# Taking the attention output and its query gradient out of one PSUM bank with one multiply

## The chip, the core and the metric

The kernel runs on one core of a Trainium2 chip. Its engines work side by side, each through its own queue in order: TensorE (PE, with its weight loads PEld), VectorE (DVE), ScalarE (ACT), GpSimd (POOL), and SyncE (SP), which here only issues transfers. SBUF is the working memory and PSUM takes what TensorE writes; GpSimd works on SBUF. The metric is the time of one execution in microseconds, the median of the runs.

## The reference

Two attention blocks work on a sequence of 2048 tokens of width 448 with 16 heads of 28, and the program returns their joined output and the gradients of all eight inputs for a given gradient of the output. Block A is linear attention. Block B, with which the change deals, has one key head and one value head for all 16 query heads:

```python
q = (x @ wq).reshape(B, S, H, Dh).transpose(0, 2, 1, 3)
k, v = x @ wk, x @ wv
scores = einsum("bhqd,bkd->bhqk", q, k) * (Dh ** -0.5)
p = softmax(scores, axis=-1)
o = einsum("bhqk,bkd->bhqd", p, v)
out_B = o.transpose(0, 2, 1, 3).reshape(B, S, H * Dh) @ wo
```

Backward, with dO the gradient of o and D the sum of dO times o over a head's width: dP = dO v^T, dS = p (dP - D), dQ = scale dS k, dK = scale dS^T q, dV = p^T dO. The inputs are bfloat16.

## The kernel before, in words

After block A and the projections of block B, a core loop does the attention of block B forward and backward. Its work is cut into 64 blocks (`NB`), each of 256 queries (`qc`) and one pair of heads. A block has eight units of 256 keys; so there are 512 units (`NU`), and the loop at line 905 runs over `u` in 540 steps, 28 more than there are units because the backward stages trail. The heads are padded to 32 rows. The order of every engine's queue is the order in which the loop writes the instructions down (`tc.manual_schedule()`): it is set by hand, with `due(u, lag)`, which returns block b when u is 8 b + lag, and None otherwise.

In step `u`, in the order of the code:

- `rows_SD` (line 663): TensorE computes the scores S of unit u for both heads into two of three score banks (`SB`), and dP minus D for unit `w = u - 16` into the two banks `DB`. The third score bank is `spare`; which it is goes in a period of four steps (line 909). D comes in through an extra row: row 0 of a padded head of dO holds minus D over the softmax's sum, and v has minus ones there.
- For even u, `o_dq` advances two accumulations in one PSUM bank, `oq`: o of unit u-2 (`o_mm`, rows 0 to 63, with a row of ones in v that gives the softmax's sum) and dQ of unit u-20 (`dq_mm`, rows 64 to 127). A second call at the end of the step does units u-1 and u-19.
- The spare bank takes, by step, the transposes of o (`onat_T`, line 788), those of dO (`don_T`), or a part of the output projection (`out_proj`).
- ScalarE computes the first head's exponential (L927), copies the second head's dP to SBUF as `cp` (L941), and computes the second exponential (L973). VectorE multiplies the first head's dP by the exponential into `dsT` (L939), GpSimd does the same with `cp` for the second head (L942).
- VectorE's small work follows, and then, last in the step, a 32x32-block transpose of the `dsT` of two steps before (L1006), which the dK products read.
- SyncE transposes four units of exponentials at a time by a transfer, `eN<-eT` (L975), for the dV products (`dv_mm`); in the units 30 to 55 of every 64, GpSimd copies queries into `qst` (L833), and SyncE transposes those (L837). In odd steps TensorE runs the dK products (`dk_m`), in some even steps four dV products of `dv_mm`.

The chain of o through a block b, with the steps at which it is written down: VectorE copies rows 0 to 63 of `oq` to `oTs` at lag 9 (L955). TensorE transposes them through the spare bank at lag 10 (L791). `o_norm` at lag 10 takes the reciprocal of the softmax's sum (L800) and multiplies by it (L801), into the first 128 columns of `oTs`; GpSimd then multiplies by dO into `prod` (L805), scales dO into `don` (L808), and writes o as bfloat16 over dO in `do_nat` (L809). `row_D` at lag 12 sums `prod` on VectorE (L813), and GpSimd puts the result into `don` (L814). At lag 14 TensorE transposes `don` (L822), VectorE copies it to `doT` (L829), and at lag 16 the products of `rows_SD` begin to read it. dQ of a block is complete two blocks later; VectorE multiplies rows 64 to 127 of `oq` by the scale and writes them over the queries at lag 27 (L958). In units of a block (u modulo 8) the copy of o is thus in unit 1, the normalising in 2, the taking out of dQ in 3, the sum in 4, and the copy of `doT` in 6. The copy of a piece of the output projection (L728) is in unit 0.

Of the kernel before, what the change touches and what calls it, by code (L numbers as in the profile page):

```python
# [25 lines left out]
def kernel(  # L26
# [604 lines left out]
    with ExitStack() as cs_:  # L631
# [59 lines left out]
        identF = pp_.tile([P, P], F32, name="identF", bufs=1)  # L691
        make_identity(nc, identF[:])
        oTs = pp_.tile([P, 256], F32, name="oTs", bufs=1)
        wo = pc_.tile([P, 4, D], BF16, name="wo", bufs=1)
# [10 lines left out]
        outs.update({456 + 8 * n: (10 + n // 2, n % 2 * (D // 2), (n % 2 + 1) * (D // 2)) for n in range(8)})  # L705
# [76 lines left out]
        onps, tps2 = {}, {}  # L782
# [5 lines left out]
        def onat_T(b, bank):  # L788
            onp = bank[:, 0:P].rearrange("p (q h c) -> p q h c", q=2, h=2)
            for qb in range(2):  # L790
                nc.tensor.transpose(onp[:, qb, :, :].rearrange("p h c -> p (h c)"), oTs[0:64, qb * P:(qb + 1) * P],  # L791
                                    identF[0:64, 0:64], tile_position=(0, 0))
            onps[b] = onp

        def o_norm(b):
            onp = onps.pop(b)
            qc, pair, g, hp = blk(b)
            r_ = pw_.tile([P, 2, 2, 1], F32, name="rl")
            os_ = oTs[:, 0:P].rearrange("p (q h c) -> p q h c", q=2, h=2)
            nc.vector.reciprocal(out=r_[:], in_=onp[:, :, :, 0:1])  # L800
            nc.vector.tensor_tensor(out=os_, in0=onp[:, :, :, :], in1=r_[:].to_broadcast([P, 2, 2, 32]), op=ALU.mult)  # L801
# [3 lines left out]
            nc.gpsimd.tensor_tensor(out=prod[b][:], in0=dnv, in1=os_, op=ALU.mult)  # L805
            dn = pw_.tile([P, 2, 2, 32], BF16, name="don", bufs=3)
            don[b] = dn
            nc.gpsimd.tensor_tensor(out=dn[:], in0=dnv, in1=r_[:].to_broadcast([P, 2, 2, 32]), op=ALU.mult)  # L808
            nc.gpsimd.tensor_copy(out=dnv, in_=os_)  # L809
# [40 lines left out]
        def o_mm(v):  # L850
            b, tp = divmod(v, 8)
            for t2 in range(2):
                t = 2 * tp + t2
                for h in range(2):
                    mmt(oq[32 * h:32 * h + 32, 0:256], vaug[:, t, :],
                        eT(v)[:, h, t2 * 256:(t2 + 1) * 256], (0, 32 * h), t == 0, t == 15)
                yield

        def dq_mm(y):
            b, tp = divmod(y, 8)  # L860
            for t2 in range(2):
# [34 lines left out]
        with tc.manual_schedule():  # L896
# [8 lines left out]
            for u in range(NU + 28):  # L905
# [29 lines left out]
                if hasD:  # L935
# [5 lines left out]
                    nc.scalar.activation(out=cp[:, :], in_=dp[1][:, :], func=ACT.Copy)  # L941
                    nc.gpsimd.tensor_tensor(out=dst[:, 1, :], in0=cp[:, :], in1=ew[:, 1, :], op=ALU.mult)  # L942
                gq, iq = divmod(u % 64 - 30, 8)
                qq = u // 64 + 1
                if 0 <= gq < 4 and u < 448:
                    if gq == 0 and iq == 0:
                        qX[qq] = (pqb_ if qq % 2 else pqa_).tile([P, 4, 2, 512], BF16, name="qX")
                    if iq < 2:
                        qc_copy(nc.gpsimd, qst, qq, gq, iq)
                if (b := due(u, 12)) is not None:  # L950
                    row_D(b)
                if u == 7:
                    nc.vector.memset(oTs[64:128, :], 0.0)
                if (b := due(u, 9)) is not None:
                    nc.vector.tensor_copy(out=oTs[0:64, :], in_=oq[0:64, 0:256])  # L955
                if (b := due(u, 27)) is not None:
                    qc, pair, g, hp = blk(b)
                    nc.vector.tensor_scalar(out=qT_B[g][64 * hp:64 * hp + 64, qc * 256:(qc + 1) * 256],  # L958
                                            in0=oq[64:128, 0:256], scalar1=scale, scalar2=None, op0=ALU.mult)
# [162 lines left out]
```

## Time and profile before

| what | us |
|---|---|
| median of 3 runs | 1068.79 |
| lowest and highest run | 1068.59, 1069.49 |
| the profiled execution | 1067.99 |
| its span | 1066.3 |
| granted clock of TensorE in it | 0.998 |
| L939, first and last start | 240.2, 1016.8 |

The views are: the page, with the busy time of each engine and the chain of work that ended last; busy time by stretch; the waits, "who <- whom: us in total, times, longest"; and the timelines of single engines, with the start and duration of every instruction in us and in brackets the idle time before it and what ended it. On VectorE, ScalarE and GpSimd an instruction can start before the one in front has ended, since its first part overlaps the other's last; so the distance from start to start is what an instruction takes from its engine, and the durations are somewhat longer. TensorE's durations overlap far more, and its 98% say little.

### The profile page before, as it was taken

The page shows a single profiled execution, that of the slowest core. Times are in us where ns is not written, and L with a number is a line of the kernel's source. Part 1 is how long each engine was busy: PE and PEld are TensorE (multiplying, and loading weights), DVE is VectorE, ACT ScalarE, POOL GpSimd, SP SyncE. Part 2 cuts the span into 40 slices and gives each one's busy share as a digit, 9 for nine tenths or more (in the row PEclk, how much of TensorE's full clock was granted, in tenths as well). Part 3 has the DMA queues.
Part 4 walks back from the last instruction along what each step waited for, and adds up shares of the span by engine and source line. Part 5 has one row for each costly group of instructions (what it writes and reads, how often), then busy time and mean ns, then how long its engine had stood idle before and what let it go on. Part 6 is the DMA issues. An engine that isn't in the chain of part 4 may idle for free.

```text
span 1066.3 us, 39861 instructions
## 1 busy us (share of the span) xinstructions
PE 1042.2 (98%) x16241; PEld 476.1 (45%) x16241; DVE 896.1 (84%) x1797; ACT 873.7 (82%) x1741; POOL 781.3 (73%) x1033
## 2 busy tenths in 40 slices
PE   9999999999999999999999999999999999999998
PEld 5555555433444444444444444444444444444434
DVE  7888400459999999999999999999999999999943
ACT  6454122479999999999999999999999999999622
POOL 6001242227988898899889989988998999888881
PEclk9999999999999999999999999999999999999999
DMA  9749899079999999999999999999999999999963
GB/s 267 163 95 200 161 214 250 21 138 168 192 202 198 170 203 187 195 191 193 196 186 189 197 192 198 185 191 194 195 195 195 195 191 186 206 191 179 218 141 92
DMA packets 689936, 195.14 MB, mean 183 GB/s; under 512 B 670616, under 2 KB 687792, under 8 KB 689752
## 3 DMA queue, kind: packets, MB, share of 16 engines
q1 hardware_dynamic: 680152, 179.92, 99.2%
q0 software_dynamic: 4640, 8.71, 2.8%
q10 hardware_dynamic: 4960, 3.96, 1.3%
q8 instruction: 127, 2.08, 0.7%
q14 instruction: 57, 0.47, 0.1%
HBM read 12.60 MB, written 10.84 MB: 22 GB/s over the span
## 4 chain that ended last, share of the span: by engine, by line
PE 52%; DVE 35%; POOL 4%; issue 4%; ACT 3%; DMA 1%; DVEq 0%; POOLq 0%; ACTq 0%
PE agen L656 20%; PE agen L81 15%; DVE dsT L939 14%; DVE dsx L1006 12%; PE aacc L656 9%; PE aacc L81 7%; POOL dsT L942 4%; DVE R L958 2%; DVE oTs L801 2%; DVE oTs L955 2%; ACT cp L941 1%; DVE rl L800 1%; ACT eT L973 1%; DMA dsx<-R 1%; ACT eT L927 0%
## 5 line engine op out<-in xcount | busy, mean ns | idle before, releaser
L942 POOL TENSOR_TENSOR dsT<-cp,eT 128x512 bf16<-128x512 bf16 x512 | 588.1, 1157 | 77.3 <-ACT cp L941 68.9
L1006 DVE STREAM_TRANSPOSE dsx<-dsT 128x512 f32<-128x512 f32 x512 | 356.4, 696 | 2.4 <-POOL dsT L942 0.2
L656 PEld LDWEIGHTS <-R 32*128 32x128 bf16 (+1 forms) x9104 | 215.5, 93 | 318.3 <-issue 293.0
L939 DVE TENSOR_TENSOR dsT<-agen,eT 128x512 bf16<-128x512 f32 x512 | 338.5, 661 | 11.7 <-PE agen L656 8.4
L941 ACT ACTIVATE cp<-agen 128x512 bf16<-128x512 f32 x512 | 324.7, 634 | 12.5 <-PE agen L656 12.5
L927 ACT ACTIVATE eT<-aacc 128x512 bf16<-128x512 f32 x512 | 324.0, 633 | 11.6 <-PE aacc L656 4.7
L973 ACT ACTIVATE eT<-aacc 128x512 bf16<-128x512 f32 x512 | 330.6, 646 | 0.0
L656 PE MATMUL agen<-doT,R 32*128 32x256 bf16 x2048 | 270.9, 269 | 10.9 <-DVE dsT L939 8.2
L656 PE MATMUL aacc<-R,R 32*128 32x256 bf16 (+1 forms) x2240 | 269.7, 268 | 2.7 <-ACT eT L927 0.8
L656 PE MATMUL agen<-dsx,qX 32*32 32x512 bf16 x4096 | 267.7, 375 | 0.0
L656 PE MATMUL agen<-eT,R 128*32 128x256 bf16 x2048 | 182.0, 276 | 0.1
L656 PE MATMUL agen<-dsT,R 128*32 128x256 bf16 x2048 | 181.4, 276 | 0.1
L656 PEld LDWEIGHTS <-qX 32*32 32x32 bf16 x4096 | 79.7, 89 | 114.9 <-issue 54.3
L656 PE MATMUL aacc<-eN,don 128*32 128x512 bf16 x1024 | 97.6, 379 | 0.0
L81 PEld LDWEIGHTS <-R 128*128 128x128 bf16 (+1 forms) x517 | 41.0, 99 | 42.9 <-issue 11.1
L406 POOL COPY pk<-R 128x256 bf16<-128x256 bf16 x4 | 1.6, 397 | 75.3 <-DVE R L366 75.3
L81 PE MATMUL agen<-R,R 128*128 128x448 bf16 (+1 forms) x180 | 42.4, 363 | 0.3 <-ACT R L225 0.3
L833 POOL COPY qst<-R 128x512 bf16<-128x512 bf16 x56 | 34.2, 611 | 4.8 <-DMA qX<-qst 4.6
L805 POOL TENSOR_TENSOR prod<-R,oTs 128x128 f32<-128x128 bf16 x64 | 27.5, 430 | 9.8 <-DVE oTs L801 9.8
L656 PEld LDWEIGHTS <-don 128*32 128x32 bf16 x1024 | 34.2, 97 | 0.8
L422 DVE TENSOR_TENSOR osb<-aacc,pr 64x448 bf16<-64x448 f32 x2 | 1.2, 617 | 37.9 <-DMA out_dram<-osb 24.0
L958 DVE TENSOR_SCALAR R<-agen 64x256 bf16<-64x256 f32 x64 | 27.3, 426 | 3.6 <-PE agen L656 1.6
(231 smaller groups left out, 971.1 us busy)
## 6 DMA issues: line engine op xcount, KB each, us to landing
out_dram<-osb ACTq DMA_DIRECT2D x22, 112.0 KB
eN<-eT SPq DMA_TRANSPOSE x128
xa<-in_A_x_dram SPq DMA_DIRECT2D x8, 224.0 KB
ga<-in_grad_out_dram SPq DMA_DIRECT2D x4, 448.0 KB
xa<-in_grad_out_dram POOLq DMA_DIRECT2D x4, 448.0 KB, 5.7
out_dram<-wdq POOLq DMA_DIRECT2D x8, 224.0 KB, 3.8
eT<-in_grad_out_dram SPq DMA_DIRECT2D x4, 448.0 KB
eT<-in_B_x_dram SPq DMA_DIRECT2D x4, 448.0 KB
```

The lines of the kernel that those rows point to most:

```text
L81: nc.tensor.matmul(out_ap, lhsT=lhsT, rhs=rhs, start=start, stop=stop, tile_position=(0, 0))
L656: nc.tensor.matmul(out, lhsT=lhsT, rhs=rhs, start=start, stop=stop, tile_position=pos, skip_group_check=True)
L801: nc.vector.tensor_tensor(out=os_, in0=onp[:, :, :, :], in1=r_[:].to_broadcast([P, 2, 2, 32]), op=ALU.mult)
L805: nc.gpsimd.tensor_tensor(out=prod[b][:], in0=dnv, in1=os_, op=ALU.mult)
L833: eng.tensor_copy(out=st.rearrange("p (b s) a j -> p b s a j", s=2)[:, :, s, :, :], in_=src.unsqueeze(2).to_broadcast([P, 4, 4, 32]))
L927: nc.scalar.activation(out=eT(u)[:, 0, :], in_=sp[0][:, :], func=ACT.Exp, scale=scale)
L939: nc.vector.tensor_tensor(out=dst[:, 0, :], in0=dp[0][:, :], in1=ew[:, 0, :], op=ALU.mult)
L941: nc.scalar.activation(out=cp[:, :], in_=dp[1][:, :], func=ACT.Copy)
L942: nc.gpsimd.tensor_tensor(out=dst[:, 1, :], in0=cp[:, :], in1=ew[:, 1, :], op=ALU.mult)
L958: nc.vector.tensor_scalar(out=qT_B[g][64 * hp:64 * hp + 64, qc * 256:(qc + 1) * 256], in0=oq[64:128, 0:256], scalar1=scale, scalar2=None, ...
L973: nc.scalar.activation(out=eT(u)[:, 1, :], in_=sp[1][:, :], func=ACT.Exp, scale=scale)
L1006: nc.vector.transpose(out=dsx[b][:, tp, :, :, :].rearrange("p h t c -> p (h t c)").bitcast(F32), in_=dsT[y][:, :, :].rearrange("p h c -> p ...
```

## The change

o is accumulated two steps later, so that o of block b and dQ of block b-2 are complete in the bank `oq` at the same step. Which half of the bank's rows each of them has changes from block to block, so that one VectorE multiply over all 128 rows takes out both at u = 8 b + 11 (unit 3), with a factor per row (`fac`: 1 for o, the scale for dQ), into `oTs`. GpSimd casts the rows of dQ from there to bfloat16 over the queries. For the last two blocks VectorE takes dQ out as before.

The transposes and the normalising of o go from lag 10 to 12 (unit 4), writing to a buffer of their own, `o_s`; the sum of `prod` goes from lag 12 to 13, ahead of GpSimd's `dsT` product of that step; GpSimd's cast of o goes from right behind `o_norm` to lag 14 (`o_keep`). The dV products of a block go from the steps 20 (two of them), 22 and 26 to 18, 20, 22 and 26. The last eight output projections and the transposing transfer of o that they need come later. The identity for the transposes of o is 64 columns wide, in both halves of the rows. `don` has two buffers instead of three.

```diff
+        o_s = pp_.tile([P, 2, 2, 32], F32, name="o_s", bufs=1)
+        fac = pp_.tile([P, 2], F32, name="fac", bufs=1)
+        nc.gpsimd.memset(fac[:, :], 1.0)
+        for n in range(2):
+            nc.gpsimd.memset(fac[64 * n:64 * n + 64, n:n + 1], scale)
...
-        outs.update({456 + 8 * n: (10 + n // 2, n % 2 * (D // 2), (n % 2 + 1) * (D // 2)) for n in range(8)})
+        outs.update({464 + 8 * n: (10 + n // 2, n % 2 * (D // 2), (n % 2 + 1) * (D // 2)) for n in range(8)})
...
         def onat_T(b, bank):
+            r = 64 * (1 - b % 2)
             for qb in range(2):
-                nc.tensor.transpose(onp[:, qb, :, :].rearrange("p h c -> p (h c)"), oTs[0:64, qb * P:(qb + 1) * P],
-                                    identF[0:64, 0:64], tile_position=(0, 0))
+                nc.tensor.transpose(onp[:, qb, :, :].rearrange("p h c -> p (h c)"), oTs[r:r + 64, qb * P:(qb + 1) * P],
+                                    identF[r:r + 64, :], tile_position=(r, 0))
...
         def o_norm(b):
-            os_ = oTs[:, 0:P].rearrange("p (q h c) -> p q h c", q=2, h=2)
+            os_ = o_s[:]
...
-            dn = pw_.tile([P, 2, 2, 32], BF16, name="don", bufs=3)
+            dn = pw_.tile([P, 2, 2, 32], BF16, name="don", bufs=2)
...
-            nc.gpsimd.tensor_copy(out=dnv, in_=os_)
+            o_nat[b] = dnv, os_
+
+        def o_keep(b):
+            nc.gpsimd.tensor_copy(out=o_nat[b][0], in_=o_nat.pop(b)[1])
...
         def o_mm(v):
-                    mmt(oq[32 * h:32 * h + 32, 0:256], vaug[:, t, :],
-                        eT(v)[:, h, t2 * 256:(t2 + 1) * 256], (0, 32 * h), t == 0, t == 15)
+                    r = 64 * (1 - b % 2) + 32 * h
+                    mmt(oq[r:r + 32, 0:256], vaug[:, t, :],
+                        eT(v)[:, h, t2 * 256:(t2 + 1) * 256], (0, r), t == 0, t == 15)
...
         def dq_mm(y):
-                    mmt(oq[64 + 32 * h:96 + 32 * h, 0:256], kn[:, t, :],
-                        dsT[y][:, h, t2 * 256:(t2 + 1) * 256], (0, 64 + 32 * h), t == 0, t == 15)
+                    r = 64 * (b % 2) + 32 * h
+                    mmt(oq[r:r + 32, 0:256], kn[:, t, :],
+                        dsT[y][:, h, t2 * 256:(t2 + 1) * 256], (0, r), t == 0, t == 15)
...
-                    o_dq((u - 2,), (u - 20,))
-                if (b := due(u, 10)) is not None:
+                    o_dq((u - 4,), (u - 20,))
+                if (b := due(u, 12)) is not None:
                     onat_T(b, spare)
...
                     nc.scalar.activation(out=cp[:, :], in_=dp[1][:, :], func=ACT.Copy)
+                    if (b := due(u, 13)) is not None:
+                        row_D(b)
                     nc.gpsimd.tensor_tensor(out=dst[:, 1, :], in0=cp[:, :], in1=ew[:, 1, :], op=ALU.mult)
+                if (b := due(u, 13)) is not None and not hasD:
+                    row_D(b)
...
+                if u % 8 == 3 and 0 <= (b := (u - 11) // 8) < NB + 2:
+                    r = 64 * (1 - b % 2)
+                    rr = slice(r, r + 64) if b < 2 else slice(0, P)
+                    if b < NB:
+                        nc.vector.tensor_scalar(out=oTs[rr, :], in0=oq[rr, 0:256], scalar1=fac[rr, b % 2:b % 2 + 1],
+                                                scalar2=None, op0=ALU.mult)
+                    if b >= 2:
+                        qc, pair, g, hp = blk(b - 2)
+                        rq = slice(64 * hp, 64 * hp + 64)
+                        if b < NB:
+                            nc.gpsimd.tensor_copy(out=qT_B[g][rq, qc * 256:(qc + 1) * 256], in_=oTs[rq, :])
+                        else:
+                            nc.vector.tensor_scalar(out=qT_B[g][rq, qc * 256:(qc + 1) * 256], in0=oq[rq, 0:256],
+                                                    scalar1=scale, scalar2=None, op0=ALU.mult)
                 if (b := due(u, 12)) is not None:
-                    row_D(b)
-                if u == 7:
-                    nc.vector.memset(oTs[64:128, :], 0.0)
-                if (b := due(u, 9)) is not None:
-                    nc.vector.tensor_copy(out=oTs[0:64, :], in_=oq[0:64, 0:256])
-                if (b := due(u, 27)) is not None:
-                    qc, pair, g, hp = blk(b)
-                    nc.vector.tensor_scalar(out=qT_B[g][64 * hp:64 * hp + 64, qc * 256:(qc + 1) * 256],
-                                            in0=oq[64:128, 0:256], scalar1=scale, scalar2=None, op0=ALU.mult)
-                if (b := due(u, 10)) is not None:
                     o_norm(b)
+                if (b := due(u, 14)) is not None:
+                    o_keep(b)
...
-                    o_dq((u - 1,), (u - 19,))
-                    b, n = divmod(u - 20, 8)
-                    for k in {0: (0, 1), 2: (2,), 6: (3,)}.get(n, ()) if 0 <= b < NB else ():
-                        dv_mm(dv_acc, b, k // 2, k % 2)
+                    o_dq((u - 3,), (u - 19,))
+                    for k, lag in enumerate((18, 20, 22, 26)):
+                        if (b := due(u, lag)) is not None:
+                            dv_mm(dv_acc, b, k // 2, k % 2)
```

More of the change, by code (lines that the diff above doesn't have):

```diff
@@ L690 @@
         qst = pp_.tile([P, 8, 4, 32], BF16, name="qst", bufs=1)[:, :, :, :]
-        identF = pp_.tile([P, P], F32, name="identF", bufs=1)
-        make_identity(nc, identF[:])
+        identF = pp_.tile([P, 64], F32, name="identF", bufs=1)
+        for n in range(2):
+            nc.gpsimd.tensor_copy(out=identF[64 * n:64 * n + 64, :], in_=identB[64 * n:64 * n + 64, 64 * n:64 * n + 64])
         oTs = pp_.tile([P, 256], F32, name="oTs", bufs=1)
+        o_s = pp_.tile([P, 2, 2, 32], F32, name="o_s", bufs=1)
+        fac = pp_.tile([P, 2], F32, name="fac", bufs=1)
+        nc.gpsimd.memset(fac[:, :], 1.0)
+        for n in range(2):
+            nc.gpsimd.memset(fac[64 * n:64 * n + 64, n:n + 1], scale)
         wo = pc_.tile([P, 4, D], BF16, name="wo", bufs=1)
@@ L781 @@
         GW = [0, 0, 4, 4, 10, 10, 16, 16, 22, 22, 28, 28, 34, 34, 40, 40, 48, 48, 56, 56, 64, 64]
-        onps, tps2 = {}, {}
+        onps, tps2, o_nat = {}, {}, {}
         def due(u, lag):
@@ L949 @@
                         qc_copy(nc.gpsimd, qst, qq, gq, iq)
-                if (b := due(u, 12)) is not None:
-                    row_D(b)
-                if u == 7:
-                    nc.vector.memset(oTs[64:128, :], 0.0)
-                if (b := due(u, 9)) is not None:
-                    nc.vector.tensor_copy(out=oTs[0:64, :], in_=oq[0:64, 0:256])
-                if (b := due(u, 27)) is not None:
-                    qc, pair, g, hp = blk(b)
-                    nc.vector.tensor_scalar(out=qT_B[g][64 * hp:64 * hp + 64, qc * 256:(qc + 1) * 256],
-                                            in0=oq[64:128, 0:256], scalar1=scale, scalar2=None, op0=ALU.mult)
-                if (b := due(u, 10)) is not None:
+                if u == 7:
+                    nc.vector.memset(oTs[:, :], 0.0)
+                if u % 8 == 3 and 0 <= (b := (u - 11) // 8) < NB + 2:
[12 more added lines that the diff above has]
+                                                    scalar1=scale, scalar2=None, op0=ALU.mult)
+                if (b := due(u, 12)) is not None:
                     o_norm(b)
+                if (b := due(u, 14)) is not None:
+                    o_keep(b)
                     if b in (15, 31, 47, 55, 63):
```

## The prediction

> **What bounds the kernel now.** I read the page first: its busy line and its chain of waits.
>
> ```profile
> PE 1042.2 (98%) x16241; PEld 476.1 (45%) x16241; DVE 896.1 (84%) x1797; ACT 873.7 (82%) x1741; POOL 781.3 (73%) x1033
> PE 52%; DVE 35%; POOL 4%; issue 4%; ACT 3%; DMA 1%; DVEq 0%; POOLq 0%; ACTq 0%
> ```
>
> No engine is alone: the chain runs half on PE, a third on VectorE. The busy time of the stretch from 600 to 700 us, in the middle of the loop (PE, PEld, DVE, ACT, POOL, then clock, DMA share, GB/s), and the SyncE row of the transposes of eT:
>
> ```profile
> 600.00:700.00 100.00, 98.83 (x1891) 43.56 (x1894) 97.21 (x190) 99.15 (x200) 90.80 (x111) 1.00 1.20 192
> L975 SPq DMA_TRANSPOSE eN<-eT x128: 4779/5427/5972, 226.8 to 992.2; - x128
> ```
>
> Four engines stand above 90%, and SyncE issues two transposes of 5.43 us per block of eight units: 10.9 us. So I need the order within a block. ScalarE's timeline gives the length of each unit (u modulo 8): the distance between two L927, the first exponentials. In the block starting at 532.47 us:
>
> ```profile
> 535.35 0.69 ACT L927 ACTIVATE eT<-aacc 128x512 bf16<-128x512 f32 x1
> ...
> 536.99 0.60 ACT L927 ACTIVATE eT<-aacc 128x512 bf16<-128x512 f32 x1
> ...
> 538.48 0.60 ACT L927 ACTIVATE eT<-aacc 128x512 bf16<-128x512 f32 x1
> ...
> 540.19 0.60 ACT L927 ACTIVATE eT<-aacc 128x512 bf16<-128x512 f32 x1
> ```
>
> Unit 2 lasts 1.64, unit 3 1.49, unit 4 1.71. The eight are 1.45, 1.43, 1.64, 1.49, 1.71, 1.45, 1.43, 1.43 (12.03); the next block, from 544.51, has 1.45, 1.49, 1.64, 1.49, 1.59, 1.45, 1.43, 1.48 (12.02). The two kinds alternate. 1.43 is ScalarE back to back, so a block loses some 0.55. Unit 2's loss stands in the list of waits:
>
> ```profile
> PEld aacc L791 <- ACT eT L973: 9.7, 46, 0.2
> ```
>
> The transposes of o write the spare score bank, which the unit before's second exponential (L973) still reads; TensorE stands still 0.2 us, once a block. Unit 4's loss is VectorE's: these are its lines in the block of 532.47 from unit 2 on, and in the next block's unit 6.
>
> ```profile
> 536.20 0.18 DVE L800 RECIPROCAL rl<-aacc 128x4 f32<-128x4 f32 x1
> 536.41 0.29 DVE L801 TENSOR_TENSOR oTs<-aacc,rl 128x128 f32<-128x128 f32 x1
> 536.62 0.70 DVE L1006 STREAM_TRANSPOSE dsx<-dsT 128x512 f32<-128x512 f32 x1
> 537.25 0.65 DVE L939 TENSOR_TENSOR dsT<-agen,eT 128x512 bf16<-128x512 f32 x1
> 537.93 0.43 DVE L958 TENSOR_SCALAR R<-agen 64x256 bf16<-64x256 f32 x1
> 538.39 0.71 DVE L1006 STREAM_TRANSPOSE dsx<-dsT 128x512 f32<-128x512 f32 x1
> 539.13 0.69 DVE L939 TENSOR_TENSOR dsT<-agen,eT 128x512 bf16<-128x512 f32 x1
> 539.74 0.28 DVE L813 TENSOR_REDUCE Dq<-prod 128x4 f32<-128x128 f32 x1
> ...
> 553.71 0.65 DVE L939 TENSOR_TENSOR dsT<-agen,eT 128x512 bf16<-128x512 f32 x1
> 554.39 0.29 DVE L829 COPY doT<-aacc 64x256 bf16<-64x256 bf16 x1
> 554.72 0.71 DVE L1006 STREAM_TRANSPOSE dsx<-dsT 128x512 f32<-128x512 f32 x1
> 555.46 0.69 DVE L939 TENSOR_TENSOR dsT<-agen,eT 128x512 bf16<-128x512 f32 x1
> ```
>
> A unit's product (L939) lags 0.26 behind its first exponential in unit 3 (537.25 against 536.99) and 0.65 in unit 4. TensorE needs that product's end before it may overwrite the bank: the next first exponential comes 1.06 after L939's start (539.13 to 540.19). A lag over 0.38 (1.06 and 0.38 are 1.44) stretches the unit.
>
> **The change, part by part.**
>
> *Take-out.* L955 (0.40) and L958 (0.43) go; one multiply of 128x256 from PSUM comes, in unit 3. L958 shows the price: 0.43; more partitions cost nothing in these rows (64x256 and 128x128 follow their columns). From start to start a plain one takes 0.33 (L955 at 534.59, transpose at 534.92). L958 costs more than its duration: it starts 0.68 after L939, where followers usually start at 0.58, and the product behind it starts 0.74 after the transpose instead of 0.62. Product to product is 1.88 there; I take the plain follower's 0.58 + 0.34 + 0.62 = 1.54 (bounds 1.54 and 1.88). Unit 1 loses its 0.33, so VectorE is relieved by some 0.67 per block, by 0.33 at least.
> Were the new multiply delayed like L958, product to product would stay 1.88; L813's own turn would come some 0.28 later, which the wait worked out below swallows, so the sum would be the same.
> The Trainium skill, "VectorE: DVE Perf Modes", section "Two Vector instructions with no wait between them", models such delays: an instruction waits for all earlier ones when it starts in another group of 32 partitions than the last read or write of that memory. L958 reads from partition 64, the new multiply from 0, so by the rule it is the 1.54.
>
> *Order of o.* Transposes and normalising move from unit 2 to unit 4, the reduction L813 from 4 to 5, ahead of that unit's GpSimd product. Unit 4 again has spare bank 2, read by unit 3's second exponential, so the 0.2 us stall moves along: unit 2 becomes 1.44, unit 3 1.45 (no spare bank to wait for), unit 4 1.64, unit 5 takes over unit 3's 1.49. Moving a value-gradient product from unit 4 to 2 balances this on TensorE: unit 4 ran two such products in 1.34 us (538.06 to 539.42, first matmul to first) against 1.52 for unit 2 (535.05 to 536.57), so unit 2 with two is ScalarE's 1.44. That product needs its eT transposes 3.2 us sooner; their landings leave at least 2.5 us. Cost nothing.
>
> *GpSimd.* Its lines around the same block:
>
> ```profile
> 536.61 1.15 POOL L942 TENSOR_TENSOR dsT<-cp,eT 128x512 bf16<-128x512 bf16 x1 [0.31 <-ACT cp L941]
> 537.72 0.43 POOL L805 TENSOR_TENSOR prod<-R,oTs 128x128 f32<-128x128 bf16 x1
> 538.12 0.40 POOL L808 TENSOR_TENSOR don<-R,rl 128x128 bf16<-128x128 bf16 x1
> 538.58 0.29 POOL L809 CAST R<-oTs 128x128 bf16<-128x128 f32 x1
> ```
>
> The new cast has 256 columns. L809 (128 columns, 0.289) and the page's L406 (256, 0.397) and L833 (512, 0.611) lie on one line, so 0.40, at most twice L809, 0.58. A unit leaves GpSimd 0.31 idle, so it fits in front of unit 4's product with nothing over. Per block GpSimd has eight products spaced 1.11, small work of about 1.4 and in half the blocks two copies of 0.57: 10.3 to 11.4, now up to 11.8 of 12.0. It is full, but catches up by unit 3.
> The skill's "Perfetto Trace Analysis", section "Optimizing GPSIMD Operations", speaks against such a move: other engines are to be preferred. By the rows the cast itself would cost nothing, were it not for what stands behind it:
>
> *The new wait.* Today L813 starts 1.45 to 1.58 after L805 has ended: two units lie between. Now one does. Let T be the start of unit 3's second exponential. By unit 1's rows (534.87, then 536.20 and 537.25) the reciprocal starts at T+1.33, unit 5's product at T+2.38; the reduction could start 0.60 later, T+2.98. But unit 4's cp starts at T+0.97 (two steps of ScalarE), GpSimd's product 0.67 to 0.76 after cp (540.69 to 541.36; 535.85 to 536.61), say T+1.68, L805 1.11 later, ending T+3.22, and a semaphore's 0.05: T+3.27. VectorE waits 0.28 (bounds: 0.2, and 0.6 if GpSimd comes late), and behind the reduction stand the transpose and unit 6's product: T+3.27+0.19+0.62 = T+4.08. Unit 6's first exponential is at T+2.12+1.49 = T+3.61, so the lag is 0.47 instead of 0.10, and unit 6 lasts 0.47+1.06 = 1.53, not 1.43. In blocks like 544.51's, unit 6's doT copy takes product to product to 1.75 (553.71 to 555.46): unit 7's product starts at T+5.83, the next exponential at T+6.89, so unit 7 lasts 1.75. In the other kind the doT copy frees the spare bank at T+4.08+0.58+0.27 = T+4.93, and from such a release to the exponential after next took 1.78 (536.70 to 538.48), less up to 0.04: unit 7 is 1.55.
> GpSimd's last piece (L814) ends near T+3.85, transposed by TensorE at about T+3.86 (in unit 6 0.22 after the first exponential): up to 0.15 of waiting, in the shadow of the product above.
>
> *Sum of units 2 to 7.* First kind: 1.44+1.45+1.64+1.49+1.53+1.55 = 9.10, before 9.15. Second: 1.44+1.45+1.64+1.49+1.53+1.75 = 9.30, before 9.08. Mean +0.085; over some 60 blocks +5.1 us. Set-up and tail cost under 1 us either way; taken as 0. The profiled execution took 1067.99 (span 1066.3 and 1.7 around it), so 1073.1; the median of the runs is 0.8 higher, within their own spread, and I stay at 1073.
>
> **Rivals.**
> *Faster.* The reduction finds L805 done. For it: L805 needs only 0.29 less time. Then unit 6's product starts at T+3.79, unit 6 lasts 1.44, unit 7 1.44 or 1.55: sums 8.90 and 9.01, mean -0.16, 60 blocks -9.6: 1058. Each 0.1 of wait costs about 0.1 a block, so the sign turns at a wait of about 0.18. Against it: the cast sits right ahead. SyncE's 10.9 us plus a 1.31 us qX transpose in half the blocks (11.5 on average) sets a floor not far below.
> *Slower still.* GpSimd is 0.2 later at unit 4 (a cast of 0.58, or late from the copies): the wait is 0.48, 0.2 more per block, +12: 1085.
> *No change.* Relief and wait cancel (wait near 0.18), or unit 4's stall was ScalarE's all along: 1068.
>
> **How the numbers follow.** My forecast 0.42 (own range 1066 to 1080), faster 0.33 (1052 to 1067), slower still 0.17, no change 0.08. The range 1056 to 1086 leaves out the tails of the second and third. A measurement tells 0.2% (2.1 us) from nothing. Faster: 0.31 of the second and 0.03 of the first; same: 0.06 of the last and 0.09 of the neighbours; the rest, 0.51, slower.
>
> **What would show it.** Right: L813 idle 0.2 to 0.3 for L805, unit 2 at 1.44, unit 4 at 1.64, units 6 and 7 longer; the multiply at 0.43, the cast at 0.40. Wrong: L813 without idle time, or idle time of L1006 behind GpSimd's L942; unit 4 at 1.45, if the bank is free sooner.

## The result, and the profile after

The changed kernel took 1081.47 us, the median of 4 runs (1080.24 to 1082.19), beside 1068.69 for the kernel before (1067.27 to 1069.49): a ratio of 1.012, with a 95% interval of 1.0102 to 1.0137. It is slower by 12.8 us; forecast was slower by some 5. The profiled execution took 1082.19, its span is 1080.1. The loop took all of it: from the first first-exponential to the last it is 785.1 us long against 770.6, while the set-up ahead of it became 1.6 shorter and the tail 0.8 longer.

The page's busy line and its chain of waits, after:

```profile
PE 1050.2 (97%) x16232; PEld 467.8 (43%) x16241; DVE 881.6 (82%) x1735; ACT 879.2 (81%) x1741; POOL 800.9 (74%) x1098
...
PE 43%; POOL 27%; ACT 15%; issue 8%; DVE 7%; POOLq 0%; ACTq 0%; DVEq 0%
```

VectorE is busy for 14.5 us less and GpSimd for 19.6 more, as the change says. But the chain, which ran a third on VectorE and 4% on GpSimd, now runs 27% on GpSimd. The stretch from 600 to 700 us (PE, PEld, DVE, ACT, POOL, clock, DMA share, GB/s):

```profile
600.00:700.00 100.00, 98.35 (x1860) 41.85 (x1856) 93.27 (x177) 97.98 (x196) 91.64 (x116) 1.00 1.19 191
```

The SyncE row of the transposes of eT (shortest, median and longest in ns):

```profile
L999 SPq DMA_TRANSPOSE eN<-eT x128: 4781/5380/6017, 225.8 to 1005.2; - x128
```

The transposes cost what they did. Of the engines GpSimd alone got busier in this stretch, by 0.8 points; the others wait more, VectorE by 3.9 points. For whom stands in the list of waits between 400 and 960 us, some 46 blocks (who <- whom: us in total, times, longest):

```profile
PEld L832 <- POOL don L824: 21.1, 45, 0.7
DVE Dq L823 <- POOL prod L812: 18.8, 45, 0.6
...
PEld aacc L798 <- ACT eT L997: 9.5, 45, 0.2
```

The last line is the old stall of the spare bank, unchanged in size. The two others now come once a block: VectorE waits for `prod` ahead of the sum (before: never), TensorE for GpSimd's last piece of `don` ahead of its transposes (before: twice, 1.0 us in all). ScalarE's timeline gives the units; the first exponentials of one block, whose unit 3 begins at 540.61:

```profile
540.61 0.69 ACT L939 ACTIVATE eT<-aacc 128x512 bf16<-128x512 f32 x1
...
542.07 0.69 ACT L939 ACTIVATE eT<-aacc 128x512 bf16<-128x512 f32 x1
...
543.71 0.60 ACT L939 ACTIVATE eT<-aacc 128x512 bf16<-128x512 f32 x1
...
545.20 0.60 ACT L939 ACTIVATE eT<-aacc 128x512 bf16<-128x512 f32 x1
...
547.00 0.60 ACT L939 ACTIVATE eT<-aacc 128x512 bf16<-128x512 f32 x1 [0.22 <-PE aacc L656]
...
548.59 0.60 ACT L939 ACTIVATE eT<-aacc 128x512 bf16<-128x512 f32 x1
...
550.04 0.62 ACT L939 ACTIVATE eT<-aacc 128x512 bf16<-128x512 f32 x1
```

Units 3 to 7 last 1.46, 1.64, 1.49, 1.80 and 1.59, unit 0 of the next block 1.45. Typical blocks of the two kinds, forecast and measured (before: the two blocks of the prediction; measured: medians of blocks 20 to 55):

| unit | 2 | 3 | 4 | 5 | 6 | 7 | sum |
|---|---|---|---|---|---|---|---|
| first kind, before | 1.64 | 1.49 | 1.71 | 1.45 | 1.43 | 1.43 | 9.15 |
| forecast | 1.44 | 1.45 | 1.64 | 1.49 | 1.53 | 1.55 | 9.10 |
| measured | 1.44 | 1.46 | 1.64 | 1.49 | 1.79 | 1.59 | 9.41 |
| second kind, before | 1.64 | 1.49 | 1.59 | 1.45 | 1.43 | 1.48 | 9.08 |
| forecast | 1.44 | 1.45 | 1.64 | 1.49 | 1.53 | 1.75 | 9.30 |
| measured | 1.44 | 1.46 | 1.64 | 1.49 | 1.57 | 1.79 | 9.39 |

One number stands out, unit 6 of the first kind. VectorE's lines from unit 3's product to unit 6's, first kind:

```profile
540.64 0.69 DVE L951 TENSOR_TENSOR dsT<-agen,eT 128x512 bf16<-128x512 f32 x1 [0.16 <-PE agen L656]
541.25 0.48 DVE L972 TENSOR_SCALAR oTs<-agen,fac 128x256 f32<-128x256 f32 x1
541.64 0.70 DVE L1030 STREAM_TRANSPOSE dsx<-dsT 128x512 f32<-128x512 f32 x1
542.27 0.66 DVE L951 TENSOR_TENSOR dsT<-agen,eT 128x512 bf16<-128x512 f32 x1
...
545.14 0.29 DVE L823 TENSOR_REDUCE Dq<-prod 128x4 f32<-128x128 f32 x1 [0.52 <-POOL prod L812]
545.34 0.70 DVE L1030 STREAM_TRANSPOSE dsx<-dsT 128x512 f32<-128x512 f32 x1
545.97 0.66 DVE L951 TENSOR_TENSOR dsT<-agen,eT 128x512 bf16<-128x512 f32 x1
```

The new multiply (L972) is harmless. The sum (L823) stands 0.52 us for GpSimd's `prod`, and behind it come the transpose and unit 6's product, 0.77 behind unit 6's first exponential (545.20); 1.03 after that product the next exponential starts. GpSimd in the same block, and then in the next one, of the second kind:

```profile
541.87 1.15 POOL L956 TENSOR_TENSOR dsT<-cp,eT 128x512 bf16<-128x512 bf16 x1 [0.32 <-ACT cp L953]
543.08 0.39 POOL L978 CAST R<-oTs 64x256 bf16<-64x256 f32 x1
543.56 1.16 POOL L956 TENSOR_TENSOR dsT<-cp,eT 128x512 bf16<-128x512 bf16 x1
544.67 0.44 POOL L812 TENSOR_TENSOR prod<-R,o_s 128x128 f32<-128x128 bf16 x1
...
554.17 1.15 POOL L956 TENSOR_TENSOR dsT<-cp,eT 128x512 bf16<-128x512 bf16 x1 [0.31 <-ACT cp L953]
555.27 0.39 POOL L978 CAST R<-oTs 64x256 bf16<-64x256 f32 x1
555.64 1.15 POOL L956 TENSOR_TENSOR dsT<-cp,eT 128x512 bf16<-128x512 bf16 x1
556.75 0.43 POOL L812 TENSOR_TENSOR prod<-R,o_s 128x128 f32<-128x128 bf16 x1
```

The cast lasts 0.39 in both. But from the product in front to the product behind it is 1.69 in the first kind and 1.47 in the second. The one difference found is the rows that it casts: 64 to 127 in the first, 0 to 63 in the second.

### The profile page after: what moved, and what is told of

Read it like the earlier page. It is cut to its first block, busy times and chain, and to the rows that moved or that the text cites. A ratio compares the mean times of both kernels' runs of the same rounds, so it can differ in the third digit from the quotient of the medians.

```text
span 1080.1 us, 39972 instructions
## 1 busy us (share of the span) xinstructions
PE 1050.2 (97%) x16232; PEld 467.8 (43%) x16241; DVE 881.6 (82%) x1735; ACT 879.2 (81%) x1741; POOL 800.9 (74%) x1098
## 4 chain that ended last, share of the span: by engine, by line
PE 43%; POOL 27%; ACT 15%; issue 8%; DVE 7%; POOLq 0%; ACTq 0%; DVEq 0%
POOL dsT L956 20%; PE agen L81 14%; PE agen L656 13%; ACT cp L953 8%; PE aacc L656 7%; PE aacc L81 7%; ACT eT L997 5%; DVE dsx L1030 3%; ACT eT L939 2%; POOL prod L812 2%; POOL R L978 1%; DVE dsT L951 1%; POOL don L815 1%; POOL qst L843 1%; PE aacc L832 1%
## 5 line engine op out<-in xcount | busy, mean ns | idle before, releaser
L656 PEld LDWEIGHTS <-R 128*32 128x32 bf16 (+1 forms) x9104 | 212.2, 93 | 313.2 <-issue 270.4
L939 ACT ACTIVATE eT<-aacc 128x512 bf16<-128x512 f32 x512 | 320.4, 626 | 20.8 <-PE aacc L656 17.3
L953 ACT ACTIVATE cp<-agen 128x512 bf16<-128x512 f32 x512 | 320.9, 627 | 12.9 <-PE agen L656 11.9
L997 ACT ACTIVATE eT<-aacc 128x512 bf16<-128x512 f32 x512 | 326.6, 638 | 0.0
L656 PE MATMUL agen<-doT,R 32*128 32x256 bf16 x2048 | 279.9, 269 | 2.9 <-DVE dsT L951 2.1
L656 PE MATMUL agen<-dsT,R 128*32 128x256 bf16 x2048 | 188.4, 276 | 0.5 <-issue 0.5
L656 PE MATMUL agen<-eT,R 128*32 128x256 bf16 x2048 | 188.3, 276 | 0.1
L823 DVE TENSOR_REDUCE Dq<-prod 128x4 f32<-128x128 f32 x64 | 18.3, 286 | 26.1 <-POOL prod L812 26.1
L812 POOL TENSOR_TENSOR prod<-R,o_s 128x128 f32<-128x128 bf16 x64 | 27.6, 432 | 11.2 <-DVE o_s L808 11.2
```

The lines of the kernel that those rows point to most:

```text
L656: nc.tensor.matmul(out, lhsT=lhsT, rhs=rhs, start=start, stop=stop, tile_position=pos, skip_group_check=True)
L823: nc.vector.tensor_reduce(out=Dq[:, :, :, 0], in_=prod[b][:], axis=AX.X, op=ALU.add)
L939: nc.scalar.activation(out=eT(u)[:, 0, :], in_=sp[0][:, :], func=ACT.Exp, scale=scale)
L997: nc.scalar.activation(out=eT(u)[:, 1, :], in_=sp[1][:, :], func=ACT.Exp, scale=scale)
```

## The experiments

Four theories were set against one another. V: VectorE's wait for `prod` ahead of the sum sets the time. T: TensorE's wait for GpSimd's last piece of `don` does. G: GpSimd is simply full, wherever its work stands. M: merging the two take-outs is worth what it takes off VectorE. Ratios are to the kernel before on the same chip, with 95% intervals; diffs are to the changed kernel unless another is named, and "..." marks left-out lines; "the sum's wait" and "TensorE's wait" are the two lines that came into the list above. Differences from the changed kernel in us are between medians from different chips, on which the kernel before took 1067.2 to 1068.7. The expectations count the experiments in the order in which they were made: the fifth is "prod first on GpSimd", the sixth "prod first, and don transposed late", the ninth "don first, then prod".

**TensorE's wait taken away.** The transposes of `don` and the copy to `doT` are written at the end of unit 6, behind its second `o_dq`.

```diff
-                if (b := due(u, 14)) is not None:
-                    don_T(b, spare)
...
-                if (b := due(u, 14)) is not None:
-                    don_copy(b)
...
                             dv_mm(dv_acc, b, k // 2, k % 2)
+                    if (b := due(u, 14)) is not None:
+                        don_T(b, spare)
+                        don_copy(b)
```

> Only TensorE's transposes of don (and the copy of doT behind them) move: in unit 6 they come behind the second pair of o and dQ products and the value-gradient product, so TensorE no longer stands still in front of them for GpSimd (21.1 us in 45 waits in the changed kernel's middle stretch). Theory V (VectorE's wait for prod decides: its product in unit 6 comes 0.3 to 0.5 us late and the next first exponential follows 1.03 behind it): units 6 and 7 stay at 1.70 and 1.69, at most 0.07 a block comes back, 1077 to 1081 us. Theory T (TensorE's own wait for GpSimd's last piece decides): unit 6 falls to 1.45 or 1.5, some 0.3 a block, 1062 us.

Measured: 1083.09, ratio 1.0137 (1.0117 to 1.0158). TensorE's wait fell from 21.1 to 6.5 us, the sum's stayed (19.4), units 6 and 7 stayed (means of blocks 20 to 55: 1.70 and 1.69, as in the changed kernel).

```profile
DVE Dq L823 <- POOL prod L812: 19.4, 46, 0.6
...
PEld L832 <- POOL don L824: 6.5, 28, 0.4
```

Most of a wait of 21 us could go and the time didn't move: it lay in the shadow of the sum's wait. T alone is out.

**The sum's wait taken away.** VectorE's block transpose of that step goes ahead of the sum, so that the sum stands last.

```diff
                     if (b := due(u, 13)) is not None:
+                        block_T(u - 18)
                         row_D(b)
...
+                if not (hasD and due(u, 13) is not None):
+                    block_T(u - 18)
```

(`block_T` holds the lines of the transpose, which are taken from the end of the step.)

> Only VectorE's order in unit 5 moves: the block transpose comes first and the sum of prod behind it, so that VectorE works 0.6 us while prod is being made; GpSimd's last piece stays where it is in its queue. Theory V: the idle time before the sum (26.1 us in 64) falls to under 4 us, unit 6 to about 1.45 and unit 7 to 1.5 or 1.6, some 0.3 a block, 1062 us. Theory T: VectorE's wait goes, but GpSimd's last piece still comes at the same time, so units 6 and 7 keep their 3.39 together, 1078 to 1082 us. If both waits end within 0.1 us of each other, this one alone gives 0.1 a block, 1075 us.

Measured: 1072.86, ratio 1.0042 (1.0027 to 1.0057), 8.6 us less than the changed kernel, between what V and T had expected. The wait is gone from the sum, unit 7 is back at 1.45; but unit 6 is 1.75, and the list of waits of this kernel says why:

```profile
PEld L832 <- POOL don L824: 27.2, 46, 1.2
```

With VectorE out of the way TensorE's wait is what is late next. Since the sum now comes 0.25 later in the second kind, the last piece, behind it, is later too.

**Both.**

> Both moves together. Theory V: the same as the sum alone, 1062 us. Theory T: the same as the transposes alone, 1062 us. If the two waits hide each other, only here does the time come back: units 6 and 7 about 2.97 to 3.04 together instead of 3.39, 0.37 a block, 1059 us.

Measured: 1069.79, ratio 1.0020 (1.0009 to 1.0031). Unit 6 is 1.46. Unit 7 is 1.72: the transposes of `don`, now last in unit 6, make VectorE's copy late (it waits 10.0 us in 44 for them). Each repair moved the loss one step on along the same chain, `prod`, sum, last piece, transposes, `doT`.

**Only the cast moved.** GpSimd's cast of dQ goes from unit 3 to unit 7, with nothing else changed.

```diff
-                        if b < NB:
-                            nc.gpsimd.tensor_copy(out=qT_B[g][rq, qc * 256:(qc + 1) * 256], in_=oTs[rq, :])
-                        else:
+                        if b >= NB:
...
+                if u % 8 == 7 and 2 <= (b := (u - 15) // 8) < NB:
+                    qc, pair, g, hp = blk(b - 2)
+                    rq = slice(64 * hp, 64 * hp + 64)
+                    nc.gpsimd.tensor_copy(out=qT_B[g][rq, qc * 256:(qc + 1) * 256], in_=oTs[rq, :])
```

> Only GpSimd's cast of dQ moves, from unit 3 to unit 7, behind the moment when prod is wanted; GpSimd has the same work. Theory V: unit 4's GpSimd product starts 0.22 us sooner in the blocks whose cast starts at row 64 and not sooner in the others, where it already starts as soon as cp is there; the wait before the sum falls from 0.59 to 0.36 in half the blocks, 0.11 a block, 1074 us. Rival G (GpSimd is simply full, wherever the work stands): 1080 to 1083 us.

Measured: 1077.29, ratio 1.0084 (1.0069 to 1.0099). This is the run that sizes the cast. Let T be the start of unit 3's second exponential, as in the prediction; medians over blocks 20 to 55:

| | unit 4's product on GpSimd | `prod` | sum | unit 6's product on VectorE |
|---|---|---|---|---|
| forecast | T+1.68 | T+2.79 | T+3.27 | T+4.08 |
| changed kernel, first kind | T+1.98 | T+3.09 | T+3.56 | T+4.39 |
| changed kernel, second kind | T+1.76 | T+2.87 | T+3.33 | T+4.16 |
| cast in unit 7, both kinds | T+1.75 | T+2.87 | T+3.33 | T+4.16 |

Without the cast both kinds stand where the second kind stood with it. So in the second kind the cast fits into the gap exactly, and costs the sum nothing; in the first kind it costs 0.22, and unit 6 of that kind falls from 1.79 to 1.56 when it goes. The rest of the sum's wait (15.0 of 18.8 us) is not the cast's: it is the order of GpSimd's queue. In the second kind unit 6 became longer in the mean (1.68 against 1.61), which takes back a part of the gain. The cast in unit 7 leaves GpSimd 0.5 later up to unit 2 there, and in one block of eight, the third with query copies (21, 29, 37, 45, 53), it hasn't caught up by unit 4: its product starts 1.18 behind `cp` instead of 0.77, and unit 6 lasts 1.93 to 1.99, against 1.56 in the others.

**prod first on GpSimd.** `prod` and `don` go ahead of unit 4's product instead of behind it.

```diff
-                    nc.gpsimd.tensor_tensor(out=dst[:, 1, :], in0=cp[:, :], in1=ew[:, 1, :], op=ALU.mult)
+                    if due(u, 12) is None:
+                        nc.gpsimd.tensor_tensor(out=dst[:, 1, :], in0=cp[:, :], in1=ew[:, 1, :], op=ALU.mult)
...
                     o_norm(b)
+                    if hasD:
+                        nc.gpsimd.tensor_tensor(out=dst[:, 1, :], in0=cp[:, :], in1=ew[:, 1, :], op=ALU.mult)
```

> Only GpSimd's order in unit 4 moves: prod and the scaled don are made ahead of that unit's dsT product, not behind it. Theory V (VectorE's wait for prod, because prod stands behind a product of 1.16 us and the cast): prod ends near 2.4 us after unit 3's second exponential, before VectorE wants it at 2.97, so the wait before the sum is gone; what is left is TensorE's wait for GpSimd's last piece, still behind the product: unit 6 about 1.59, unit 7 1.44 to 1.5 (now 1.70 and 1.69), 0.34 a block, 1061 us. Rival G (GpSimd is full, order does not matter): the same work in another order, 1078 to 1082 us, with the idle time on another engine's line.

Measured: 1064.80, ratio 0.9966 (0.9952 to 0.9979): 16.7 us less than the changed kernel, faster than before. The sum starts at T+2.96 in both kinds, without a wait, though GpSimd does the same work, cast included; in a block of the first kind (T is 537.14):

```profile
539.13 0.43 POOL L812 TENSOR_TENSOR prod<-R,o_s 128x128 f32<-128x128 bf16 x1
...
540.10 0.27 DVE L823 TENSOR_REDUCE Dq<-prod 128x4 f32<-128x128 f32 x1
```

G is out, and this is what settles V: TensorE's wait is nearly what it was, so the gain is the sum's wait. Unit 7 is back at 1.45; unit 6 is 1.58, by TensorE's wait:

```profile
PEld L832 <- POOL don L824: 19.5, 46, 0.7
```

**prod first, and don transposed late.**

> prod first on GpSimd, and TensorE's transposes of don behind the value-gradient product as in the first of the earlier experiments. Theory V with TensorE's wait next in line: unit 6 1.44, unit 7 about 1.5, period 11.9 instead of 12.33 and 12.06 before: 1056 us, under the kernel before. If the limit is GpSimd's or SyncE's work as a whole: not under 1061 us.

Measured: 1067.50, ratio 0.9994 (0.9983 to 1.0004): a miss. Unit 6 is 1.45, but unit 7 is 1.67, since the transposes again come too late for the copy to `doT`:

```profile
DVE doT L839 <- PE aacc L832: 10.0, 46, 0.4
```

The same with the cast in unit 7 too:

> The sixth experiment with the cast of dQ moved from unit 3 to unit 7. Theory V: with prod ahead of the product the cast's place no longer matters to the sum, so within 2 us of the sixth, 1054 to 1058 us. Rival (the cast in unit 3 still delays unit 4's product, and through it the last piece of don): some 5 us faster than the sixth.

Measured: 1067.93, ratio 0.9996 (0.9988 to 1.0005): the second miss, by the same cause (unit 7 at 1.69, the same wait at 9.6 us). Moving TensorE's transposes back is the wrong end; what they wait for has to come sooner.

**The merge undone, the new order kept.** In unit 3 VectorE copies o and scales dQ in two instructions, and GpSimd casts nothing.

```diff
+                    rr = slice(r, r + 64)
...
-                        nc.vector.tensor_scalar(out=oTs[rr, :], in0=oq[rr, 0:256], scalar1=fac[rr, b % 2:b % 2 + 1],
-                                                scalar2=None, op0=ALU.mult)
+                        nc.vector.tensor_copy(out=oTs[rr, :], in_=oq[rr, 0:256])
...
-                            nc.gpsimd.tensor_copy(out=qT_B[g][rq, qc * 256:(qc + 1) * 256], in_=oTs[rq, :])
...
+                        nc.vector.tensor_scalar(out=qT_B[g][rq, qc * 256:(qc + 1) * 256], in0=oq[rq, 0:256],
+                                                scalar1=scale, scalar2=None, op0=ALU.mult)
```

> Only the merge is undone: in unit 3 VectorE copies o and, in a second instruction, scales dQ straight into the queries, and GpSimd's cast is gone; the later o, the sum at lag 13 and all orders stay. Theory V: VectorE is some 0.45 us later into unit 4, but it would have waited for prod anyway: unit 4 or 5 loses 0.1 to 0.3, the wait before the sum shrinks to nothing, 1078 to 1088 us; so the merge bought next to nothing where it stands. Rival M (the merge is worth VectorE's 0.43 us a block, and the cast costs nothing): 1105 us or more. Rival G (the cast filled GpSimd): 1070 us or less.

Measured: 1086.07, ratio 1.0173 (1.0158 to 1.0189). VectorE's lines in unit 3 of this kernel:

```profile
542.24 0.69 DVE L951 TENSOR_TENSOR dsT<-agen,eT 128x512 bf16<-128x512 f32 x1 [0.16 <-PE agen L656]
542.85 0.41 DVE L973 COPY oTs<-agen 64x256 f32<-64x256 f32 x1
543.27 0.43 DVE L977 TENSOR_SCALAR R<-agen 64x256 bf16<-64x256 f32 x1
543.73 0.71 DVE L1027 STREAM_TRANSPOSE dsx<-dsT 128x512 f32<-128x512 f32 x1
544.47 0.69 DVE L951 TENSOR_TENSOR dsT<-agen,eT 128x512 bf16<-128x512 f32 x1
```

Product to product is 2.23, with the merge 1.63: it does relieve VectorE by 0.60 a block, 37 us over 62 blocks. The time shows some 5 of these. Units 4 and 5 are 1.81 and 1.79 here, but 6 and 7 are 1.45 and 1.47, and nothing waits for `prod`: a VectorE that is late itself finds it done. The changed kernel wins 0.46 in units 4 and 5 (1.64 and 1.50 in the mean), and gives 0.47 back in 6 and 7 (1.70 and 1.69). M holds for VectorE's time and falls for the kernel's.

**don first, then prod, then unit 4's product; the cast in unit 7.** Beyond the edits already shown, in `o_norm`:

```diff
-            nc.gpsimd.tensor_tensor(out=prod[b][:], in0=dnv, in1=os_, op=ALU.mult)
...
             nc.gpsimd.tensor_tensor(out=dn[:], in0=dnv, in1=r_[:].to_broadcast([P, 2, 2, 32]), op=ALU.mult)
+            nc.gpsimd.tensor_tensor(out=prod[b][:], in0=dnv, in1=os_, op=ALU.mult)
```

> On the fifth experiment (prod ahead of unit 4's product): GpSimd scales don before it makes prod, since don only needs the reciprocal, and the cast of dQ goes to unit 7, so that GpSimd is free 0.4 us sooner; TensorE's transposes of don stay in their place. Theory V with TensorE's wait next in line: GpSimd's last piece ends near 3.7 us after unit 3's second exponential instead of 4.0, before TensorE wants it at 3.86; unit 6 falls from 1.58 to 1.45 and unit 7 stays at 1.45, some 0.13 a block, 1057 us. Rival (something else holds unit 6, the score bank or GpSimd's full queue): 1064 us as the fifth.

Measured: 1063.32, ratio 0.9955 (0.9941 to 0.9970), beside the 0.9966 of prod first alone a gain too small for the intervals. TensorE's wait is down to 4.1 us in 8, units 6 and 7 are 1.49 and 1.47 in the mean, and most blocks last 11.79 and 11.93, as expected. But single blocks during and behind the query copies last 12.2 to 13.6, and two lines of the list of waits (of the whole execution) that were small in the changed kernel (0.9 us in 2 and 1.3 in 1) go with them:

```profile
DVE dsx L1035 <- POOL dsT L957: 9.4, 12, 1.3
...
POOL qst L843 <- DMA qX<-qst: 8.3, 7, 2.1
```

GpSimd stands before its copy into the single buffer `qst`, since SyncE hasn't yet sent the previous transfer from it, and VectorE then stands for GpSimd's product. With the cast in unit 1 instead of 7:

> The same with the cast of dQ in unit 1 of the next block, where GpSimd has idle time in every block. Theory V: 1056 to 1058 us, as the ninth, or 1 to 2 us less if the ninth's GpSimd is late in the blocks with the copies of queries.

Measured: 1065.67, ratio 0.9982 (0.9970 to 0.9993). No better: the first kind of block is 11.87 long, the other 12.36, with units 4 and 5 at 1.76 and 1.65, and `qst` waits still (6.3 us in 5 between 400 and 960).

**Only the dV products, on the kernel before.** The diff is to the kernel before:

```diff
-                    for k in {0: (0, 1), 2: (2,), 6: (3,)}.get(n, ()) if 0 <= b < NB else ():
-                        dv_mm(dv_acc, b, k // 2, k % 2)
+                    for k, lag in enumerate((18, 20, 22, 26)):
+                        if (b := due(u, lag)) is not None:
+                            dv_mm(dv_acc, b, k // 2, k % 2)
```

> The kernel before with one part of the change alone: the value-gradient products at the steps 18, 20, 22 and 26 instead of 20 (two), 22 and 26. By the reading of the profile before, unit 4 waits for VectorE and not for TensorE, so it gains nothing there, and unit 2, which has the transposes of o and their stall, gets a third piece and grows by 0.2 (0.21 for four such products): 1068 to 1082 us. If unit 4's loss was TensorE's two products: 1062 us or less.

Measured: 1069.64, ratio 1.0024 (1.0012 to 1.0036). Unit 2 went from 1.63 to 1.85, unit 4 from 1.65 to 1.52. So the move alone costs 0.2% where the transposes of o are still in unit 2. Unit 4's gain does not show a loss of TensorE's: from VectorE's product in unit 4 to the next first exponential it is 1.06 with both pieces of dV in that unit and 1.07 with one (medians). What shrank is VectorE's lag behind the first exponentials, from 0.25 to 0.04 in unit 3, and in unit 4 from 0.65 to 0.51 in the first kind and from 0.52 to 0.38 in the second: the longer unit 2 lets VectorE catch up. Unit 4's loss before was VectorE's, as the prediction read it.

**The query transfer ahead of the exponentials'.** The diff is to the kernel with don and prod first and the cast in unit 7:

```diff
                     nc.scalar.activation(out=eT(u)[:, 1, :], in_=sp[1][:, :], func=ACT.Exp, scale=scale)
+                    if 0 <= gq < 4 and iq == 1 and u < 448:
+                        qc_T(qst, qq, gq)
                     if u % 4 == 3:
                         nc.sync.dma_start_transpose(ENs[u // 4 % 6][:, :, :],
                                                     ETs[u // 4 % 5][:, :, :, :].rearrange("p a b c -> p (a b c)"))
-                    if 0 <= gq < 4 and iq == 1 and u < 448:
-                        qc_T(qst, qq, gq)
```

> The version with don and prod ahead of GpSimd's product and the cast in unit 7 took 1063.3, though its undisturbed blocks last 11.86; some blocks during and behind the query copies last 0.5 to 1.7 longer. Here the transfer qX<-qst is issued ahead of the transpose of eT of the same step instead of behind it, so it leaves the queue 5.4 us sooner, and nothing else is changed. If GpSimd's copy into the single buffer qst, waiting for that transfer (8.3 us in 7 there), is what disturbs the blocks, this wait goes to under 1 us and the time falls by about 5 to 1057 to 1059. If the queue as a whole is too full (two transposes of 5.43 and one of 1.3 with the gaps between them in a block of 11.9), the eT transposes come 1.3 late instead, TensorE waits for them in the dV products, and the time stays at 1062 to 1065.

Measured: 1059.20, the median of 6 runs (1056.89 to 1063.77), ratio 0.9921 (0.9903 to 0.9938), whose interval lies just clear of the 0.9941 to 0.9970 of the version without this edit. This is the fastest version, 8.8 us below the kernel before. The wait of `qst` is gone from the list, in which TensorE's wait for the last piece has become small:

```profile
PEld L832 <- POOL don L824: 2.8, 5, 0.6
```

Blocks 20 to 55 last 11.95 in the mean, 11.86 in the first kind and 12.04 in the second. The eT transposes, now behind the 1.3 us of the query transfer, made TensorE wait once between 400 and 960 us, for 0.8 us.

## Why the prediction was right or wrong

Right: slower, by the new wait in front of the sum, and inside the range of 1056 to 1086. Wrong: its size, 12.8 us instead of about 5, above the forecast's own 1066 to 1080.

*Take-out.* 1.54 from product to product was forecast, with 1.88 at the other end; measured 1.63 (0.61 to the multiply, 0.39 for it, 0.63 behind the transpose). Near the end taken: the multiply lasts 0.48, not 0.43, and is not held, as the rule in the Trainium skill's "VectorE: DVE Perf Modes", section "Two Vector instructions with no wait between them", would have it for an instruction that starts at partition 0, as its neighbours do; the scaling from partition 64 in the kernel with two take-outs is followed by the slow pattern again (0.74 behind the transpose). The 0.09 cost nothing: units 3 to 5 last what was forecast, and the sum's own turn, T+2.96, is no later than the T+2.98 of the forecast.

*Order of o and the dV products.* Units 2 to 5 came out within 0.02. "Cost nothing" for the moved dV product was right where the transposes of o had left unit 2; the run with that move alone shows 0.22 in unit 2 where they had not. In the same run unit 4 is 0.13 shorter, but through VectorE's smaller lag, so the reading that unit 4's loss before was VectorE's holds. (By the two times beside it, the prediction's 1.34 us for unit 4 on TensorE is 1.36; nothing hangs on it.)

*GpSimd: the step that failed.* "It fits in front of unit 4's product with nothing over" holds for the blocks that cast rows 0 to 63 and not for the others. The cast's duration was right (0.39 against 0.40). What was left out is that it takes its engine for longer when it starts at another partition than its neighbours: 1.22 from the product to the cast and 0.47 to the next, instead of 1.10 and 0.37. That is 0.22 in half the blocks, or 0.11 a block of the 0.19 worked out below; that the rows which it casts are the cause is inferred, as the last section says. The row that could have told it was in the prediction, on another engine: L958, from partition 64, with 0.10 in front and 0.12 behind.

*The new wait.* The sum could start at T+2.98 by the forecast, and does at T+2.96 when `prod` is there. Forecast was T+3.27; measured T+3.33 in the second kind, by 0.77 from `cp` to the product where 0.71 was taken from rows of 0.67 to 0.76, and T+3.56 in the first. So the wait was 0.37 and 0.60 instead of 0.28. The bounds, 0.2 and 0.6, held both; the lower part was taken. "Each 0.1 of wait costs about 0.1 a block" was right: units 6 and 7 together are 0.30 above the forecast in the first kind and 0.08 in the second, for 0.31 and 0.08 that unit 6's product came later. Both kinds together make 0.19 a block: 0.11 by the cast and 0.08 by the 0.77 in place of 0.71, together 11.4 us over 60 blocks on top of the forecast 5.1. The loop grew by 14.6 in all, 1.9 less than these 16.5, in part because the last eight blocks grew by 0.09 each only, and because unit 1, which the sum leaves out, is 0.03 shorter in the mean.

*TensorE's wait for the last piece* was put at up to 0.15 and in the shadow. In the shadow is right, by the first experiment; it measured 0.47, and it is what is late next as soon as the sum's wait goes.

*The rivals.* "Slower still" (GpSimd 0.2 later at unit 4, 1085) describes what happened in half the blocks, though not by a longer cast, which lasts 0.39. "Faster" asked that the sum find `prod` done and gave 1058: with `prod` first on GpSimd the sum finds it done, and the time is 1064.8, since that case left out TensorE's wait for the last piece. With that mended too, and the query transfer ahead, it is 1059.2. "No change" had the wait near 0.18; of the 64 idle times before the sum two are 0.16 and 0.17, two are 0, and all others 0.21 or more.

GpSimd as such was not the bound. The Trainium skill's "Perfetto Trace Analysis", section "Optimizing GPSIMD Operations", prefers other engines; here the version that leaves VectorE to do the cast's work was the slowest (1086.07), and another order of GpSimd's queue, with the same work, was worth 16.7 us.

## What to carry to other kernels

Where four engines stand above 90%, price a moved step by the place in each queue at which its consumer finds it: write down, from one fixed instant of the block, when each instruction of the chain can start, and ask which engine waits in order behind it. When a wait on such a chain goes, look at once for the next one along it (here VectorE's, then TensorE's, then a transfer's), since each was hidden by the one in front; and try moving the producer up in its queue before moving the consumer back. A single buffer that a full queue must empty first is part of that chain too.

## What the runs showed of the hardware that had not been expected

GpSimd loses time at a cast that starts at another partition than its neighbours, by the same amount in four kernels: the 64x256 cast of rows 64 to 127 between two products from partition 0 starts 1.219 us after the product in front and the next starts 0.474 later (the changed kernel, 31 casts), 1.219 and 0.474 (the fastest version, where it stands in unit 7), 1.223 and 0.475 (only the cast moved), 1.226 and 0.475 (the cast in unit 1); for rows 0 to 63 the first distance is 1.101, 1.100, 1.098 and 1.102, and the second 0.371 in the changed kernel and 0.357 with the cast in unit 1, where the next product isn't kept by `cp`. The duration is 0.39 in each case, so the groups by line don't show it. All 31 casts of rows 64 to 127 are slow and none of the 31 others. It goes with the rows and not with the kind of block: with the cast in unit 1 of the next block the slow ones fall into the other kind. That it is the starting partition is inferred; casts that start elsewhere were not tried.

SyncE's order matters though its transfers are not waited for in most blocks: in a block with a query transfer, that and two transposes of 5.4 us fill it for some 12 us of 11.9, and the order of two transfers issued in one step was worth 0.3% of the whole time.
